# A new order for the first ten microseconds: q on one queue, f1id and w1's first piece on the other, longer warm-up with fillers, and the first filter visits at slots 4, 7, 10 and 13

## The chip, the cores and the metric

The kernel runs on one core of one Trainium2 chip. The metric is the device time of one execution in microseconds (us). The engines are named as the profile names them: PE (TensorE matmuls), PEld (its weight loads), DVE (VectorE), ACT (ScalarE), POOL (GpSimd) and SP (SyncE). DMAs are issued here from SP, ACT and POOL; "SPq" and "ACTq" are rows of DMA issues.

## The reference

Two branches read q, and their sum is added to q. `A` is a gated long convolution, `B` a two-layer perceptron with a Mish between the layers.

```python
x = A_q                                    # 1 x 2048 x 448
xn = _layernorm(x, axis=-1)
# _A_ref(xn, k, v, shift_k, ssm_k, ssm_D): 4-tap causal conv of k, times v,
# then a causal convolution over 2048 steps (by FFT) with ssm_k, plus kv * ssm_D, times xn
# _B_ref(xn, w1, b1, w2): h = xn @ w1 + b1 (448 -> 1792); act = mish(h); act @ w2 (1792 -> 448)
return x + _A_ref(xn, A_k, A_v, A_shift_k, A_ssm_k, A_ssm_D) + _B_ref(xn, B_w1, B_b1, B_w2)
```

## The kernel before, in words

**The perceptron sets the order.** The 2048 tokens are cut into 8 chunks of 256 (`NCHUNK`), the 1792 hidden columns into 7 groups of 256 (`NP`). One chunk with one group is a *pair*, 56 in all, chunk by chunk. Each matrix is kept as a high part and a low part (`w1h`/`w1l`, `w2h`/`w2l`, `XH`/`XL`, `ach`/`acl`), and each product is the sum of high x high, high x low and low x high. Pair i is worked in two *slots*: in slot 2i its first product (`g1_mm`, line 465, 22 matmuls), in slot 2i+1 its Mish and the split of the result (`mish`, lines 473, 74 and 75), followed on PE by the second product of pair i-2 (`g2_mm`, lines 490 to 492, 12 matmuls). The engines run what they are given in the order of the code.

**Chunk 0 splits the weights.** During chunk 0 each pair needs a new piece of w1 and, two pairs later, of w2. They come by DMA into a pool of four buffers (`kr`), where a load waits until an earlier piece has been split. `w1_hi` (ACT, line 342) writes the high part, `w1_lo` (lines 347 and 349, DVE) the low part; `split` (lines 74 and 75) does the same for w2. The p-th piece of w1 is split in slot 2p-2, the p-th piece of w2 after slot 2p+3.

**The convolution is sewn in by tables.** Its first Fourier stage takes 16 *visits*: 8 for the filter h (`H_AT`, slot of each) and 8 for k times v (`KV_AT`). A visit is `f1_mm` (line 125, 8 matmuls into two `pc` buffers in PSUM, of which there are two), then `f1_fold` (line 131: a copy by ACT; lines 132 and 134: an add and a subtract by DVE), and three slots later `f1_out` (line 140: two DMAs issued by ACT to the scratch `Dh` or `Dkv`). Where work is due in the same slot, the order of the tables' loops decides.

**The head** is what runs before slot 0, written by hand at lines 595 to 636. PE runs three warm-up matmuls that depend on constants alone. The two 128-token halves of chunk 0 of q are loaded: the first half by a 64-partition DMA from SP and one from ACT, the second by ACT. Then ACT issues `f1id` (the first stage's matrix and the identity for transposes), SP the first filter tile (h's group 1), w1's first piece in two parts, w1's second piece, `b1`, and h's group 2. DVE makes the statistics of each half (`stats`, `aggr`, `eps`), POOL the reciprocal root (`power`), DVE the normalized half (`norm`, `tail`). PE runs the visit of h's group 1 (`H_HEAD`) and then transposes each half (line 426); ACT writes `XH` (line 438), DVE `XL` (line 436). POOL makes the low part of the first part of w1's first piece. The visit's fold stands in slot 0 and its output in slot 3.

Of the kernel before, what the change touches and what calls it, by code (L numbers as in the profile page):

```python
# [7 lines left out]
F32 = mybir.dt.float32  # L8
# [7 lines left out]
NJ = 16  # L16
# [5 lines left out]
EPS = 1e-5  # L22

G2_LAG = 2
H_HEAD = 1
H_AT = {2: 4, 3: 8, 0: 12, 4: 16, 5: 20, 6: 26, 7: 32}
KV_AT = (24, 29, 34, 39, 44, 50, 55, 60)
H0_AT = 63
OCT_AT = (65, 3)
I2_AT = {98: (6, 7), 102: (0, 1), 106: (2, 3), 111: (4, 5)}  # L30
LATE = 2
WARM = 3
WARM_N = 448


@with_exitstack
def tile_kernel(ctx: ExitStack, tc, q, k, v, sk, hT, sD, w1, b1, w2, c_f1, c_g, c_gi, c_i2, out):
# [53 lines left out]
    def at(slot, fn, *args):  # L91
        plan.setdefault(int(slot), []).append((fn, args))
# [16 lines left out]
    def h_load(g, eng=None):  # L109
        HT[g] = xt()  # L110
        (eng or nc.sync).dma_start(HT[g], hT[:, 2 * g:2 * g + 2])
        if g == 0:
            dt = xt()[0:1, 0]
            nc.sync.dma_start(dt, sD)
            SD.append(dt)


    def f1_mm(src, g, key):
        x = src.pop(g)
        PS[key, g] = ps = [pc(), pc()]  # L120
        for b in range(2):
            for h in range(2):
                for jj in range(2):
                    rg = 32 * (2 * b + h)
                    nc.tensor.matmul(ps[h][64 * jj:64 * jj + 64, b, :D], f1[rg:rg + 32, 0:64], x[rg:rg + 32, jj],  # L125
                                     start=True, stop=True, tile_position=(rg, 64 * jj))
# [200 lines left out]
    RW = {}  # L327


    def w1_load(p, parts=((0, 2),)):  # L330
        if ("1", p) not in RW:
            RW["1", p] = kr().rearrange("p a b -> p (a b)").rearrange("p (n a b) -> p n a b", n=2, a=4)
        for a, b in parts:
            nc.sync.dma_start(RW["1", p][:, a:b], w1[p, :, a:b])

    def w1_parts(p, a, b):
        f = lambda t: t[:, :, 256 * p + 128 * a:256 * p + 128 * b].rearrange("p k (n b) -> p k n b", b=128)
# [27 lines left out]
    def ln_load(c, eng=None):  # L365
        Q[c] = mp.tile([128, 2, D], F32, name="qt", tag="qt", bufs=3)
        if c:
            nc.sync.dma_start(Q[c], q[:, 2 * c:2 * c + 2])
        else:
            for jj in range(2):  # L370
                for h, e in ((0, nc.sync), (64, nc.scalar)) if jj == 0 else ((0, nc.scalar),):
                    n = 128 if jj else 64
                    e.dma_start(Q[c][h:h + n, jj], q[h:h + n, jj])

    def ln_parts(c):
        st = mp.tile([128, 2, 6], F32, name="bst", bufs=2)
# [127 lines left out]
    def mlp_slot(s):  # L504
        i, half = divmod(s, 2)
        n = len(pairs)
        j = i - G2_LAG
        if half == 0:
            if i < n:
                c, p = pairs[i]  # L510
                if c + 1 < NCHUNK:
                    if p == 0:
                        ln_load(c + 1)
                    if p == (2 if c else 3):
                        ln_stats(c + 1)
                    if c == 0 or p == NP - 3:
                        dv(len(drip))
                    if p == NP - 2:
                        ln_norm(c + 1)
                    if p == NP - 1:  # L520
                        ln_T(c + 1, 1)
                g1_mm(i)
        else:
            if i < n:
                c, p = pairs[i]
                if p == NP - 2 and c + 1 < NCHUNK:
                    ln_T(c + 1, 0)
                mish(i)
            if 0 <= j < n - 1:
                g2_mm(j)  # L530
            elif j == n - 1:
                for jj in range(2):
                    g2_mm(j, (jj,))
                    g2_evac(pairs[j][0], (jj,))
# [3 lines left out]
    nslots = 2 * (len(pairs) + G2_LAG)  # L538

    for g, t in H_AT.items():  # L540
        if g != 2:
            at(t - 5 if t > 7 else t - 3, h_load, g)
        if g == 0:
            after(t - 2, lambda: V.tensor_add(HT[0][0:1, 0], HT[0][0:1, 0], SD.pop()))
        at(t, f1_mm, HT, g, "h")
        after(t, f1_fold, g, "h")
        at(t + 3, f1_out, Dh, g, "h")
# [49 lines left out]
    one = cp.tile([128, NJ], F32, name="one")  # L597
    V.memset(one, 1.0)
    ve0 = cp.tile([128, 2], F32, name="ve0")
    warm = g2p.tile([128, 512], F32, name="pg2")  # L600
    for _ in range(WARM):
        nc.tensor.matmul(warm[0:NJ, 0:WARM_N], one, one[:, 0:1].to_broadcast([128, WARM_N]), start=True, stop=True)
    ln_load(0)

    nc.scalar.activation(ve0, mhalf, AF.Mish)
    ve1 = cp.tile([128, 2], F32, name="ve1")
    nc.gpsimd.tensor_tensor(ve1, one[:, 0:2], mhalf, op=ALU.pow)
    nc.scalar.dma_start(f1id, c_f1)
    h_load(H_HEAD)
    w1_load(0, ((0, 1), (1, 2)))  # L610
    w1_load(1)
    nc.sync.dma_start(b1t, b1)
    h_load(2)
    stats, aggr, eps, power, norm, tail = ln_parts(0)
    for jj in range(2):
        stats(jj)
        aggr(jj)
        eps(jj, jj + 1)
        power(jj, jj + 1)
    f1_mm(HT, H_HEAD, "h")  # L620
    w1_hi(0, 0, 1)
    w1_lo(0, 0, 1, (nc.gpsimd, None))
    ps = [g2p.tile([128, 512], F32, name="pg2") for _ in range(2)]
    x_tiles(0)
    for jj in range(2):
# [1 line left out]
        tail(jj, jj + 1)  # L627
        transposes(0, jj, ps[jj])
        x_split(0, jj, ps[jj], 0)
    w1_hi(0, 1, 2)  # L630
    x_split(0, 0, ps[0], 1)
    w1_lo(0, 0, 1, (None, V))
    x_split(0, 1, ps[1], 1)
    w1_lo(0, 1, 2)
    plan2.setdefault(0, []).append((f1_fold, (H_HEAD, "h")))
    plan.setdefault(3, []).insert(0, (f1_out, (Dh, H_HEAD, "h")))
    for s in range(nslots):
        j = s // 2 - G2_LAG - 1
        if s % 2 == 0 and j >= 0 and pairs[j][1] == NP - 1:
# [69 lines left out]
```

## Time and profile before

| | us |
|---|---|
| median of 3 timed runs | 379.8 (379.71 to 380.72) |
| the profiled execution, its own time | 379.97 |
| its span, first to last instruction | 377.9 |
| PE busy | 364.6 (96%) |
| DVE busy | 266.6 (71%) |
| ACT busy | 177.1 (47%) |
| first matmul of pair 0 starts | 12.50 |

The span lies 2.1 us under the time of its own execution. Times inside the run are counted from the span's start. In a row of the timeline the first number is the start, the second the length, then the engine, the line of the code, the operation, the tile written and the tiles read, the number of instructions, and in brackets how long the engine had been idle before and what ended that.

### The profile page before, as it was taken

Reading aid. Unit: us, or ns where it says so; the run is one execution under the profiler, and the core shown is the slowest. Engines: PE = TensorE matmul, PEld = TensorE weight load, DVE = VectorE, ACT = ScalarE, POOL = GpSimd, SP = SyncE. Lnnn points to the kernel's source line nnn. Section 1 sums busy time; section 2 is a strip of 40 time slices with the busy share of each in tenths; the row PEclk is TensorE's granted clock in tenths of the full one; section 3 lists DMA queues with packets and bytes.
Section 4 is the critical chain, followed back from the end, with each engine's and each line's share of the span. In section 5 each row is a group of like instructions: output and inputs, shape, how many; then the busy total and the mean of one; then the engine's idle time right before and its main releaser. Section 6 shows DMA issues by size and latency. Waiting matters only on the chain.

```text
span 377.9 us, 7967 instructions
## 1 busy us (share of the span) xinstructions
PE 364.6 (96%) x3382; PEld 295.0 (78%) x3382; DVE 266.6 (71%) x355; ACT 177.1 (47%) x298; POOL 25.1 (7%) x42
## 2 busy tenths in 40 slices
PE   5999999999999999999999999999999999999993
PEld 1788888978888988988886666666666889888982
DVE  2889758999999998997434747654564822997741
ACT  2677743454334433533453646456555435224540
POOL 2101000000020001000010000110000012111110
PEclk9899999999999999999999999999999999999999
DMA  7799986839488427513875498878494468739927
GB/s 265 269 310 337 378 309 178 250 85 298 116 293 216 112 52 256 152 46 97 258 254 192 143 300 225 251 256 237 129 305 121 117 182 329 260 122 295 199 63 145
DMA packets 31987, 79.38 MB, mean 210 GB/s; under 512 B 2897, under 2 KB 18130, under 8 KB 31954
## 3 DMA queue, kind: packets, MB, share of 16 engines
q1 hardware_dynamic: 20754, 47.22, 36.8%
q10 hardware_dynamic: 9328, 22.50, 22.6%
q0 software_dynamic: 1872, 9.18, 8.9%
q8 instruction: 26, 0.43, 0.5%
q14 instruction: 7, 0.06, 0.0%
HBM read 50.44 MB, written 28.44 MB: 209 GB/s over the span
## 4 chain that ended last, share of the span: by engine, by line
PE 86%; DMA 4%; DVE 3%; ACT 3%; issue 1%; ACTq 1%; SPq 0%
PE pg L465 34%; PE pg L490 12%; PE pg L491 11%; PE pg L492 11%; PE pc L199 7%; PE pc L244 4%; PE pc L125 4%; PE pg L426 2%; PE pc L302 2%; DMA f1id<-in_c_f_dram 2%; DMA Dkv<-st 1%; DMA av<-Dkv 1%; ACT a L473 1%; DVE st L132 1%; ACT XH L438 0%
## 5 line engine op out<-in xcount | busy, mean ns | idle before, releaser
L473 ACT ACTIVATE a<-pg,b1t 128x256 f32<-128x256 f32 x112 | 47.1, 472 | 107.0 <-PE pg L465 88.3
L465 PE MATMUL pg<-XH,w1h 128*128 128x256 f32 x448 | 91.2, 285 | 0.7 <-ACT XH L438 0.7
L490 PE MATMUL pg<-w2h,ach 128*128 128x448 f32 x224 | 83.3, 372 | 0.2 <-DVE qt L497 0.2
L465 PEld LDWEIGHTS pg<-XH,w1h 128*128 128x128 f32 x448 | 69.7, 188 | 17.7 <-issue 15.1
L491 PE MATMUL pg<-w2l,ach 128*128 128x448 f32 x224 | 81.4, 363 | 0.6 <-DVE w2l L75 0.6
L492 PE MATMUL pg<-w2h,acl 128*128 128x448 f32 x224 | 81.4, 363 | 0.0
L75 DVE TENSOR_TENSOR acl<-a,ach 128x512 fp32r<-128x512 f32 x56 | 38.4, 687 | 58.0 <-ACT ach L74 57.8
L465 PE MATMUL pg<-XL,w1h 128*128 128x256 f32 x448 | 69.7, 277 | 0.2 <-DVE XL L436 0.2
L465 PEld LDWEIGHTS pg<-XL,w1h 128*128 128x128 f32 x448 | 59.4, 188 | 0.3 <-DVE XL L436 0.3
L465 PE MATMUL pg<-XH,w1l 128*128 128x256 f32 x336 | 56.9, 278 | 0.0
L490 PEld LDWEIGHTS pg<-w2h,ach 128*128 128x128 f32 x224 | 42.0, 187 | 12.7 <-issue 9.8
L465 PEld LDWEIGHTS pg<-XH,w1l 128*128 128x128 f32 x336 | 46.9, 188 | 0.0
L491 PEld LDWEIGHTS pg<-w2l,ach 128*128 128x128 f32 x224 | 42.1, 188 | 3.5 <-DVE w2l L75 1.2
L492 PEld LDWEIGHTS pg<-w2h,acl 128*128 128x128 f32 x224 | 42.1, 188 | 2.7
L74 ACT CAST ach<-a 128x512 fp32r<-128x512 f32 x56 | 34.7, 620 | 1.8
L163 DVE TENSOR_TENSOR x<-x 128x896 f32<-128x896 f32 x24 | 26.2, 1091 | 0.8
L438 ACT CAST XH<-pg 128x512 fp32r<-128x512 f32 x16 | 9.4, 588 | 30.2 <-PE pg L426 29.1
L436 DVE TENSOR_TENSOR XL<-pg,XH 128x512 fp32r<-128x512 f32 x16 | 11.0, 688 | 16.8 <-ACT XH L438 16.7
L393 POOL TENSOR_TENSOR shift<-mv,mone 128x2 f32<-128x2 f32 x7 | 2.8, 396 | 280.1 <-DVE mv L385 280.1
L131 ACT COPY st<-pc 128x896 f32<-128x896 f32 x16 | 14.5, 909 | 13.4 <-PE pc L125 13.3
L125 PE MATMUL pc<-x,f1id 32*64 32x448 f32 x256 | 17.3, 585 | 3.3 <-DMA f1id<-in_c_f_dram 3.3
L252 ACT COPY qe<-pc 128x896 f32<-128x896 f32 x16 | 13.7, 911 | 13.5 <-PE pc L244 13.0
(66 smaller groups left out, 396.5 us busy)
## 6 DMA issues: line engine op xcount, KB each, us to landing
Dh<-st ACTq DMA_DIRECT2D x16, 448.0 KB, 5.3
Dkv<-st ACTq DMA_DIRECT2D x16, 448.0 KB, 5.1
ah<-Dh SPq DMA_DIRECT2D x8, 896.0 KB, 6.9
av<-Dkv SPq DMA_DIRECT2D x8, 896.0 KB, 6.7
E<-qe ACTq DMA_DIRECT2D x16, 448.0 KB, 4.9
e<-E POOLq DMA_DIRECT2D x7, 896.0 KB, 8.7
kr<-in_k_dram SPq DMA_DIRECT2D x10, 448.0 KB, 6.9
x<-in_hT_dram SPq DMA_DIRECT2D x8, 448.0 KB, 6.1
```

What stands on the lines that cost most here:

```text
L74: nc.scalar.copy(h, raw)
L75: V.tensor_sub(l, raw, h)
L125: nc.tensor.matmul(ps[h][64 * jj:64 * jj + 64, b, :D], f1[rg:rg + 32, 0:64], x[rg:rg + 32, jj], start=True, stop=True, tile_position=(rg, ...
L131: nc.scalar.copy(st[:, 1], o)
L163: V.tensor_add(KV[g], KV[g], o)
L199: nc.tensor.matmul(p[32 * t:32 * t + 32, r, :D], g[rs, t, c], a[rs, t], start=True, stop=True, tile_position=(64 * r, 32 * t))
L244: nc.tensor.matmul(ps[t // 2][cg:cg + 32, t % 2, :D], gi[ts, r, c, 32 * jj:32 * jj + 32], Y[o][c][ts, r], start=c == 0, stop=c == 1, tile_ ...
L465: nc.tensor.matmul(ps[:, n], l, r, start=n_ == 0, stop=n_ == len(mm) - 1)
L473: nc.scalar.activation(a[:, n], ps[:, n], AF.Mish, bias=b1t[:, 2 * p + n:2 * p + n + 1])
L490: nc.tensor.matmul(ps, ah[:, n, cs], w2h[:, f], start=f == 0, stop=False)
L491: nc.tensor.matmul(ps, ah[:, n, cs], w2l[:, f], start=False, stop=False)
L492: nc.tensor.matmul(ps, al[:, n, cs], w2h[:, f], start=False, stop=f == NF - 1)
```

## The change

In the head, SP now issues both halves of chunk 0 of q, each as one DMA of 128 partitions. ACT issues `f1id` and the first part of w1's first piece; SP issues the second part behind q. The filter tile of group 1 moves behind `b1` in SP's queue. The visit of group 1 leaves the head: `H_AT` now puts groups 1, 2, 3 and 0 at slots 4, 7, 10 and 13; they stood in the head and at slots 4, 8 and 12. The warm-up is four matmuls of 448 columns and one of 128; after the transposes of the first half a filler matmul of 64 columns runs, after those of the second half two of 128. The warm-up writes a `pc` buffer, no longer a `pg2` buffer. Both parts of w1's first piece are cast by ACT before `XH`, and both low parts are made by DVE. The load of chunk 1 of q moves from slot 0 to slot 2.

```diff
-H_HEAD = 1
-H_AT = {2: 4, 3: 8, 0: 12, 4: 16, 5: 20, 6: 26, 7: 32}
+H_AT = {1: 4, 2: 7, 3: 10, 0: 13, 4: 16, 5: 20, 6: 26, 7: 32}
...
-WARM = 3
-WARM_N = 448
+WARM = (448,) * 4 + (128,)
+FILL = ((64,), (128, 128))
...
             for jj in range(2):
-                for h, e in ((0, nc.sync), (64, nc.scalar)) if jj == 0 else ((0, nc.scalar),):
-                    n = 128 if jj else 64
-                    e.dma_start(Q[c][h:h + n, jj], q[h:h + n, jj])
+                nc.sync.dma_start(Q[c][:, jj], q[:, jj])
...
-                    if p == 0:
+                    if p == (0 if c else 1):
                         ln_load(c + 1)
...
-        if g != 2:
-            at(t - 5 if t > 7 else t - 3, h_load, g)
+        if g != 1:
+            at(t - 5 if t > 7 else t - 4, h_load, g)
...
-    warm = g2p.tile([128, 512], F32, name="pg2")
-    for _ in range(WARM):
-        nc.tensor.matmul(warm[0:NJ, 0:WARM_N], one, one[:, 0:1].to_broadcast([128, WARM_N]), start=True, stop=True)
+    warm = pc()
+
+    def heat(ns):
+        for n in ns:
+            nc.tensor.matmul(warm[0:NJ, 0, 0:n], one, one[:, 0:1].to_broadcast([128, n]), start=True, stop=True)
+
+    heat(WARM)
     ln_load(0)
-
+    nc.scalar.dma_start(f1id, c_f1)
+    w1_load(0, ((0, 1, nc.scalar), (1, 2, nc.sync)))
...
-    nc.scalar.dma_start(f1id, c_f1)
-    h_load(H_HEAD)
-    w1_load(0, ((0, 1), (1, 2)))
     w1_load(1)
     nc.sync.dma_start(b1t, b1)
-    h_load(2)
+    h_load(1)
...
-    f1_mm(HT, H_HEAD, "h")
     w1_hi(0, 0, 1)
-    w1_lo(0, 0, 1, (nc.gpsimd, None))
+    w1_hi(0, 1, 2)
...
         x_split(0, jj, ps[jj], 0)
-    w1_hi(0, 1, 2)
+        heat(FILL[jj])
+    w1_lo(0, 0, 1)
     x_split(0, 0, ps[0], 1)
-    w1_lo(0, 0, 1, (None, V))
     x_split(0, 1, ps[1], 1)
     w1_lo(0, 1, 2)
-    plan2.setdefault(0, []).append((f1_fold, (H_HEAD, "h")))
-    plan.setdefault(3, []).insert(0, (f1_out, (Dh, H_HEAD, "h")))
```

What stands on an engine in a row is shown at three places; the changed kernel's line numbers are 3 or 4 lower behind the edits. First SP's queue at the start, before (`qt` is q, `x` a filter tile, `kr` a piece of w1 or w2, `b1t` the bias):

```order
L373 DMA qt<-in_q_dram 64x448
L111 DMA x<-in_hT_dram 128x896
L334 DMA kr<-in_w_dram 128x512 x2
L334 DMA kr<-in_w_dram 128x1024
L612 DMA b1t<-in_b_dram 128x14
L111 DMA x<-in_hT_dram 128x896
```

The same place after the change:

```order
L370 DMA qt<-in_q_dram 128x448 x2
L333 DMA kr<-in_w_dram 128x512
L333 DMA kr<-in_w_dram 128x1024
L611 DMA b1t<-in_b_dram 128x14
L110 DMA x<-in_hT_dram 128x896
L356 DMA kr<-in_w_dram 128x896
```

The filter tile that stood second has moved behind the bias, and both halves of q stand first. Second, DVE from the end of the head to the split of pair 0, before (`w1h` and `w1l` in lines 347 and 349 are the low parts of w1, `st` is the fold of a visit, `acl` the low part of a Mish result):

```order
L436 TENSOR_TENSOR XL<-pg_145,XH 128x4x128
L349 TENSOR_TENSOR w1h<-kr,w1h 64x128
L436 TENSOR_TENSOR XL<-pg_146,XH 128x4x128
L347 TENSOR_TENSOR w1l<-kr,w1h 128x3x128
L349 TENSOR_TENSOR w1h<-kr,w1h 64x128
L347 TENSOR_TENSOR w1l<-kr,w1h 128x3x256
L349 TENSOR_TENSOR w1h<-kr,w1h 64x256
L132 TENSOR_TENSOR st<-pc,st 128x896
L134 TENSOR_TENSOR st<-pc,st 128x896
L75 TENSOR_TENSOR acl<-a,ach 128x512
```

The same place after the change:

```order
L346 TENSOR_TENSOR w1l<-kr,w1h 128x3x128
L348 TENSOR_TENSOR w1h<-kr,w1h 64x128
L433 TENSOR_TENSOR XL<-pg_134,XH 128x4x128
L433 TENSOR_TENSOR XL<-pg_135,XH 128x4x128
L346 TENSOR_TENSOR w1l<-kr,w1h 128x3x128
L348 TENSOR_TENSOR w1h<-kr,w1h 64x128
L346 TENSOR_TENSOR w1l<-kr,w1h 128x3x256
L348 TENSOR_TENSOR w1h<-kr,w1h 64x256
L74 TENSOR_TENSOR acl<-a,ach 128x512
```

One more low part of w1 stands ahead of the two `XL`, and the two operations of a fold are gone from ahead of `acl`. Third, DVE between the low parts of w2's second piece (p = 1) and third piece (p = 2), before:

```order
L75 TENSOR_TENSOR w2l<-kr,w2h 128x896
L347 TENSOR_TENSOR w1l<-kr,w1h 128x3x256
L349 TENSOR_TENSOR w1h<-kr,w1h 64x256
L382 BN_STATS bst<-qt 128x6 x2
L385 BN_AGGR mv<-bst 128x2 x2
L388 TENSOR_SCALAR ve<-mv 128x2
L75 TENSOR_TENSOR acl<-a,ach 128x512
L75 TENSOR_TENSOR w2l<-kr,w2h 128x896
```

The same place after the change:

```order
L74 TENSOR_TENSOR w2l<-kr,w2h 128x896
L346 TENSOR_TENSOR w1l<-kr,w1h 128x3x256
L348 TENSOR_TENSOR w1h<-kr,w1h 64x256
L379 BN_STATS bst<-qt 128x6 x2
L382 BN_AGGR mv<-bst 128x2 x2
L385 TENSOR_SCALAR ve<-mv 128x2
L74 TENSOR_TENSOR acl<-a,ach 128x512
L131 TENSOR_TENSOR st<-pc,st 128x896
L133 TENSOR_TENSOR st<-pc,st 128x896
L74 TENSOR_TENSOR w2l<-kr,w2h 128x896
```

The fold of the visit at slot 7 (group 2) now stands between them. Before, a fold stood in slots 0, 4, 8 and 12; now one stands in slots 4, 7, 10 and 13.

More of the change, by code (lines that the diff above doesn't have):

```diff
@@ L327, in tile_kernel, with w1_load @@
     RW = {}
-    def w1_load(p, parts=((0, 2),)):
+    def w1_load(p, parts=((0, 2, nc.sync),)):
         if ("1", p) not in RW:
             RW["1", p] = kr().rearrange("p a b -> p (a b)").rearrange("p (n a b) -> p n a b", n=2, a=4)
-        for a, b in parts:
-            nc.sync.dma_start(RW["1", p][:, a:b], w1[p, :, a:b])
+        for a, b, eng in parts:
+            eng.dma_start(RW["1", p][:, a:b], w1[p, :, a:b])
     def w1_parts(p, a, b):
```

## The prediction

> **What bounds the kernel now.** The page comes first. Its busy times and its 40 slices (9.4 us each, digits are tenths) show a PE that is full from the second slice to the last but one.
>
> ```profile
> PE 364.6 (96%) x3382; PEld 295.0 (78%) x3382; DVE 266.6 (71%) x355; ACT 177.1 (47%) x298; POOL 25.1 (7%) x42
> ...
> PE   5999999999999999999999999999999999999993
> ```
>
> So the time is PE's stream of work, plus what PE waits for. The change touches the first slice and the spacing of the visits up to slot 13; I read that stretch only. The timeline, PE's rows, first: warm-up, the head's visit, the transposes, the first matmul of pair 0, the first wait of the second product, the first matmul of pair 3.
>
> ```profile
> 1.00 4.17 PE L602 MATMUL pg<-one 128*16 128x448 f32 x6 [1.00 <-DVE one L598]
> ...
> 8.43 1.80 PE L125 MATMUL pc<-x,f1id 32*64 32x448 f32 x16 [3.26 <-DMA f1id<-in_c_f_dram]
> 10.17 1.66 PE L426 MATMUL pg<-f1id,xn 128*128 128x128 f32 x8
> 12.50 0.62 PE L465 MATMUL pg<-XH,w1h 128*128 128x256 f32 x3 [0.68 <-ACT XH L438]
> ...
> 23.06 0.47 PE L491 MATMUL pg<-w2l,ach 128*128 128x448 f32 x1 [0.63 <-DVE w2l L75]
> ...
> 25.37 0.52 PE L465 MATMUL pg<-XH,w1h 128*128 128x256 f32 x3
> ```
>
> Pair 0 starts at 12.50. What it waits for stands in DVE's and POOL's rows.
>
> ```profile
> 3.77 0.63 DVE L382 BATCH_NORM_STATS2 bst<-qt 128x6 f32<-128x448 f32 x1 [2.82 <-DMA qt<-in_q_dram]
> ...
> 7.64 0.63 DVE L382 BATCH_NORM_STATS2 bst<-qt 128x6 f32<-128x448 f32 x1 [2.85 <-DMA qt<-in_q_dram]
> ...
> 9.55 1.18 DVE L404 TENSOR_SCALAR xn<-qt,mv,rstd 128x448 f32<-128x448 f32 x1 [0.22 <-POOL rstd L394]
> 10.76 0.20 DVE L408 COPY xn<-xn 128x64 f32<-128x64 f32 x1
> ```
>
> ```profile
> 8.76 0.75 POOL L394 TENSOR_TENSOR rstd<-ve,mhalf 128x1 f32<-128x1 f32 x1 [3.33 <-DVE ve L388]
> 9.48 1.00 POOL L347 TENSOR_TENSOR w1l<-kr,w1h 128x384 fp32r<-128x384 f32 x1
> ```
>
> The second half of q ends the head. It is there at 7.64; then come statistics, POOL's root, the second half's normalization (1.18 us, beside POOL's 1.00 us of low part; the same instruction takes 0.51 us for the first half), its tail to 10.96, transposes, ACT's cast, pair 0: 12.50 - 7.64 = 4.86 us.
>
> ```profile
> 8.60 0.51 DVE L404 TENSOR_SCALAR xn<-qt,mv,rstd 128x448 f32<-128x448 f32 x1
> ```
>
> Last, the chain of waits gives PE's units where nothing is late: a first product is 2.51 us, a visit 0.94, and the second product what lies between, 53.46 - 51.06 = 2.40.
>
> ```profile
> 48.55 2.51 PE pg L465 x22
> ...
> 53.46 0.94 PE pc L125 x16
> ```
>
> **Part 1: when q is there.** ACT issued the second half early, and it landed 6.2 us later.
>
> ```profile
> 0.75 1.46 ACTq L373 DMA_DIRECT2D qt<-in_q_dram  x2
> ...
> 1.37 0.56 SPq L111 DMA_DIRECT2D x<-in_hT_dram  x1
> ```
>
> ```profile
> qt<-in_q_dram ACTq DMA_DIRECT2D x1, 224.0 KB, 6.2
> ```
>
> Why: from 3.5 to 4 us the DMA engines served one queue alone, and that was the larger one, SP's, with the filter tile. ACT's queue has no row there.
>
> ```profile
> q1 hardware_dynamic: 32, 0.11, 74.4%
> ```
>
> In the changed order the two halves of q (448 KB, 459 kB in thousands of bytes) have only `f1id` (128 KB, 131 kB) beside them: 590 kB. The rates at that time are the last number of these rows:
>
> ```profile
> 2.00:3.00 1.00, 1.00 (x2) 0.15 (x1) 0.00 (x0) 0.76 (x1) 0.00 (x0) 1.00 1.04 253
> 3.00:4.00 1.00, 1.00 (x3) 0.18 (x2) 0.23 (x1) 0.73 (x2) 0.00 (x0) 1.00 0.84 203
> 4.00:5.00 1.00, 1.00 (x3) 0.11 (x1) 0.73 (x3) 0.00 (x0) 0.12 (x1) 1.00 0.87 312
> ```
>
> 253 + 203 = 456 kB by 4.0, the other 134 at 312 by 4.43. From the last byte to the start of the statistics I take 0.55 us; for the first half before (229 kB, by 2.91, used at 3.77) the same sum gives 0.86, with other bytes mixed in. So the second half is used at 5.0 (an estimate; 4.6 if the two queues mix less, 5.8 in a rival below) and not at 7.64.
>
> **Part 2: from q to pair 0.** The 4.86 us shrink in two places. POOL no longer makes a low part beside the normalization: 1.18 becomes 0.51, so -0.67. And the transposes: before, eight took 1.66 us at half clock. PE's granted clock (the third number from the end; PE's busy time is the first after the length) shows why:
>
> ```profile
> 4.55:7.97 3.42, 0.63 (x2) 0.00 (x0) 0.54 (x3) 0.14 (x1) 0.55 (x1) 1.00 1.02 376
> 7.97:11.38 3.41, 2.95 (x22) 1.58 (x23) 2.63 (x7) 0.55 (x2) 1.72 (x2) 0.50 1.04 402
> 11.38:14.79 3.41, 2.58 (x20) 2.15 (x19) 2.73 (x6) 3.35 (x5) 0.00 (x0) 1.00 0.52 210
> ```
>
> A stretch with 0.63 of 3.42 us busy was followed by clock 0.50; one with 2.95 busy was followed by 1.00. After the change the warm-up ends near 6.0 (six passes took 4.17 us; 8.5 are issued, the later ones at full clock), and the transposes of the first half and a filler come at 6.7: about 2.3 of the 3.42 us are busy. That is nearer to the 2.58 after which the clock stayed than to 0.63, so I take full clock: the last four transposes take 0.4 and not 0.8 us, -0.3. Rest: 4.86 - 0.67 - 0.3 = 3.9. Pair 0 starts at 5.0 + 3.9 = 8.9, **-3.6 us**. The visit that leaves the head costs nothing there: the transposes that count are those of the second half, at 11.0, after it. The casts of w1 by ACT and the extra low part on DVE (384 columns on POOL in 1.00 us, less on DVE) lie in the wait for the transposes and the cast; without that cover they would cost up to 1 us. The Trainium skill (TensorE: Matmul & The Clock Gate, The HAM clock gate) says that the half rate returns after an idle window of some 3.4 us; the trace shows it returning after a window that was not idle, 18% busy, so the trace is stricter, and the fillers have a purpose.
>
> **Part 3: the visit in the stream.** The visit of group 1 ran while PE had nothing else. At slot 4 it is in the full stream: **+0.94**.
>
> **Part 4: the stretch up to pair 3.** From 12.50 to 25.37 are 12.87 us. Three first products, a visit and a second product are 7.53 + 0.94 + 2.40 = 10.87, so 2.0 us are lost. The fold of the head's visit and its output stand in this stretch: ACT issues the output's two DMAs just ahead of the Mish of pair 1.
>
> ```profile
> 18.18 1.31 ACTq L140 DMA_DIRECT2D Dh<-st  x2
> ...
> 19.54 0.84 ACT L473 ACTIVATE a<-pg,b1t 128x256 f32<-128x256 f32 x2 [1.30 <-PE pc L125]
> ...
> 21.91 1.09 DVE L75 TENSOR_TENSOR w2l<-kr,w2h 128x896 fp32r<-128x896 f32 x1 [0.15 <-ACT w2h L74]
> ```
>
> Then come the split, the cast of w2, and at 23.00 the low part on which PE waits (the row at 23.06). With fold and output gone from here, that chain is, from the end of pair 1: 0.2 to start (an estimate), 21.91 - 19.54 = 2.37 for Mish, split and cast, 1.09 for the low part = 3.66; PE has a visit, a first product and one matmul (0.94 + 2.51 + 0.20 = 3.65) to do in that time. It fits. What stays is 0.2 for `XL` in pair 0 (DVE makes an extra low part first) and 0.1 at each change of shape: 0.5. **-1.5.**
>
> **Part 5: the new wait.** Between the ends of the low parts of w2's pieces 0 and 2, DVE took, before,
>
> ```profile
> 24.36 1.09 DVE L132 TENSOR_TENSOR st<-pc,st 128x896 f32<-128x896 f32 x1
> 25.48 1.09 DVE L134 TENSOR_TENSOR st<-pc,st 128x896 f32<-128x896 f32 x1
> ...
> 31.64 1.08 DVE L75 TENSOR_TENSOR w2l<-kr,w2h 128x896 fp32r<-128x896 f32 x1
> ```
>
> 32.72 - 23.00 = 9.7 us with one fold. After the change two folds (slots 4 and 7) stand there: 9.7 + 2.2 = 11.9. PE needs, in the same time, the rest of a second product (2.2), two first products, a visit, a second product and one matmul: 2.2 + 5.02 + 0.94 + 2.40 + 0.2 = 10.8. So pair 2's second product waits about 1.1 us for `w2l`, and with it everything on PE behind it; 1.3 with the changes of shape. Before, the stretch from 25.37 to 36.59 (11.22 us for 5.02 + 4.80 + 0.94 = 10.76) lost 0.46. **+0.85.**
>
> Behind slot 13 both kernels have done the same visits, and the tables are the same.
>
> **Sum.** -3.6 + 0.94 - 1.5 + 0.85 = -3.3 us, from the profiled execution's 379.97 to 376.7; from the median, 379.8, to **376.5**.
>
> **Rivals.** *The queues share evenly.* Then `f1id` and w1's first part (384 KB, 393 kB) move beside q: 852 kB; 768 by 5.0, the rest at 312 by 5.27, used at 5.8. That is 0.8 later: 377.3. For it: both of ACT's transfers are now issued at the start. Against it: the half microsecond in which ACT's queue had no byte. The Trainium skill (DMA: Bandwidth & Descriptors, Issuing engines are not separate DMA queues) says that transfers of all issuers run on the same 16 engines and interleave, so that a second issuer saves issue time only; by that rule alone the sum is this rival's. The same page (Queues, rings and completion order) has each engine drain a whole packet of one ring before it turns to the next, which agrees with the row at 3.5 us.
>
> *The clock stays at half* to 11.38, as before. The last transposes take 0.4 more, pair 0 starts at 9.3, and its first 2.1 us run at half rate, 1.05 lost: +1.45, 377.95. It decides if 2.3 busy us of a window are too few, or the window falls otherwise.
>
> *The load stream is the bound.* The DMA share (last but one) is near full behind the head:
>
> ```profile
> 12.50:25.37 12.87, 12.09 (x94) 10.56 (x95) 11.41 (x17) 10.40 (x17) 0.00 (x0) 1.00 0.77 258
> 25.37:36.59 11.22, 11.22 (x85) 9.69 (x84) 10.99 (x18) 7.86 (x12) 1.71 (x3) 1.00 0.97 330
> 36.59:48.39 11.80, 11.80 (x94) 10.49 (x92) 9.20 (x12) 9.07 (x16) 0.00 (x0) 1.00 0.99 368
> ```
>
> If loads set the pace, they come earlier only by idle time that goes: 0.23 x 12.87 = 3.0 us in the first row. With half of it kept (buffers come free no sooner), the gain is 1.5: 378.3. Against it: PE is busy all through the two rows below.
>
> *Slower: w1's fifth piece.* ACT casts it in slot 6, in front of the Mish of pair 3, the cast of w2's third piece and so the `w2l` of part 5.
>
> ```profile
> 20.15 0.33 SPq L334 DMA_DIRECT2D kr<-in_w_dram  x1
> ...
> 26.98 1.05 ACT L342 CAST w1h<-kr 128x1024 fp32r<-128x1024 f32 x1 [1.12 <-DMA kr<-in_w_dram]
> ```
>
> Before, it took 6.8 us, and ACT waited 1.12. It is issued when DVE frees its buffer, 7.65 us behind the start of pair 0; now about 6.7, since a fold no longer stands ahead: 15.6. ACT wanted it at 26.98 - 1.12 = 25.86, 13.4 behind pair 0; now, by part 4, 1.5 less: 20.8. DVE is behind by then, which gives some 0.6 of grace (an estimate); from 21.4 each us of lateness is a us of PE. At 6.8 us again that is 1.0 (377.5, within my range); slower than 379.8 by 0.3% needs a landing 10.2 us or more after the issue (25.8, 4.4 us past 21.4). The longest load of that pool before took 8.8:
>
> ```profile
> DMA to landing us min/median/max: 3.7/6.3/8.8
> ```
>
> *It does not do what it says:* the second half of q comes no sooner. Then pair 0 starts at 7.64 + 3.9 = 11.5, -1.0, and the sum is -0.7: 379.1, no change to be told. Against it: q is first in its queue.
>
> **Chances.** Forecast 0.55, even queues 0.15, clock 0.12, loads 0.07, slower 0.03, no sooner 0.08. A difference of 0.3%, 1.1 us, is about what a measurement can tell from none. Faster: the first four, 0.89; same 0.08; slower 0.03. Range: below, 4.6 for q and half of the new wait (-0.4 - 0.55), so 375.5; above, the clock's 378.0 with w1's or the loads' case beyond it: 375.5 to 378.2.
>
> **What would show it.** In the changed profile: DVE's second statistics at 4.6 to 5.3; its second normalization 0.5 us; transposes 0.1 us apart; pair 0 at 8.6 to 9.4 with clock 1.00; no ACT wait ahead of the Mish of pair 1; a PE wait of about 1 us on `w2l` in pair 2's second product, some 19 us behind the start of pair 0; SP's third to sixth loads without gaps. I am wrong if pair 0 starts after 10, or if PE loses over 2 us between pair 0 and slot 13.

## The result and the profile after

The changed kernel took 376.8 us (median of 4 runs, 376.71 to 376.92). The kernel before, run beside it, took 380.26 (379.71 to 381.4). The ratio is 0.9905, with a 95% interval of 0.988 to 0.9931: 3.5 us sooner, where 376.5 was forecast. The profiled execution is the one of 376.92, with a span of 374.9; it is compared below with the profiled execution of before (379.97, span 377.9). Two single executions among all the runs, one of 1252.29 us of the kernel before and one of 920.61 us in experiment 6, stand far outside and enter no ratio.

The page: PE's first slice now reads 8 and not 5, and the rest of the row is as full as it was.

```profile
PE 365.5 (97%) x3392; PEld 295.5 (79%) x3392; DVE 266.1 (71%) x356; ACT 176.9 (47%) x298; POOL 23.8 (6%) x41
...
PE   8999999999999999999999999999999999999993
```

DVE's rows of the head: statistics of the first half, statistics of the second half, normalization of the second half.

```profile
3.92 0.63 DVE L379 BATCH_NORM_STATS2 bst<-qt 128x6 f32<-128x448 f32 x1 [2.96 <-DMA qt<-in_q_dram]
...
4.96 0.63 DVE L379 BATCH_NORM_STATS2 bst<-qt 128x6 f32<-128x448 f32 x1
...
6.86 0.51 DVE L401 TENSOR_SCALAR xn<-qt,mv,rstd 128x448 f32<-128x448 f32 x1 [0.22 <-POOL rstd L391]
```

The row at 4.96 has no bracket: DVE came straight from its own work on the first half, which ended at 4.94. q had only just landed. Its second half was issued at 1.17, and the longer of the two landings of q took 3.8 us (3.76 in the trace, so 4.93):

```profile
DMA to landing us min/median/max: 3.1/3.5/3.8
```

So the landing and DVE met within 0.01 us, and from there on the chain runs through DVE. What the DMA engines moved up to then stands in the next rows: the rate in two stretches (last number), and SP's queue (q1) and ACT's (q10) from 0 to 4.43 us, in packets, MB and share of the engines' time.

```profile
3.00:4.00 1.00, 1.00 (x3) 0.18 (x2) 0.09 (x1) 0.17 (x1) 0.00 (x0) 1.00 1.07 388
4.00:5.00 1.00, 1.00 (x4) 0.31 (x3) 0.92 (x4) 0.00 (x0) 0.00 (x0) 1.00 1.06 388
...
q1 hardware_dynamic: 284, 0.46, 35.8%
q10 hardware_dynamic: 232, 0.31, 18.8%
```

SP's queue had begun the last packets of q's 0.46 MB by 4.43. In the same time ACT's had come to 0.31 MB: `f1id` (0.13) and 0.18 of w1's first part.

PE's rows: the warm-up, the transposes of each half (four in 0.66 us, against 1.12 at half clock in experiment 1), pair 0, pair 3, the wait in pair 2's second product, the visit at slot 10.

```profile
1.00 4.92 PE L601 MATMUL pc<-one 128*16 128x448 f32 x10 [1.00 <-DVE one L595]
6.46 0.66 PE L423 MATMUL pg<-f1id,xn 128*128 128x128 f32 x4 [0.55 <-DVE xn L401]
...
7.42 0.66 PE L423 MATMUL pg<-f1id,xn 128*128 128x128 f32 x4
...
8.75 0.63 PE L462 MATMUL pg<-XH,w1h 128*128 128x256 f32 x3
...
20.21 0.52 PE L462 MATMUL pg<-XH,w1h 128*128 128x256 f32 x3
...
29.62 0.47 PE L488 MATMUL pg<-w2l,ach 128*128 128x448 f32 x1 [0.38 <-DVE w2l L74]
...
32.03 1.01 PE L124 MATMUL pc<-x,f1id 32*64 32x448 f32 x16
```

The table of windows, cut where the clock's record has its boundaries (the clock is the third number from the end): both stretches of the head are at 1.00.

```profile
4.08:7.49 3.41, 2.78 (x14) 1.02 (x13) 2.98 (x10) 1.57 (x3) 1.30 (x2) 1.00 1.05 350
7.49:10.90 3.41, 3.28 (x24) 2.68 (x25) 3.29 (x8) 1.79 (x3) 0.00 (x0) 1.00 0.92 369
```

ACT's rows: the casts of w1's first part, and the Mish of pair 1.

```profile
5.30 1.29 ACT L341 CAST w1h<-kr 128x512 fp32r<-128x512 f32 x2 [2.14 <-DMA kr<-in_w_dram]
...
14.28 0.84 ACT L470 ACTIVATE a<-pg,b1t 128x256 f32<-128x256 f32 x2
```

The Mish has no wait ahead of it, as part 4 asked, and the casts are over before the transposes of the first half end. SP's third to sixth loads stand without a gap, as asked; later ones do not:

```profile
1.64 0.90 SPq L333 DMA_DIRECT2D kr<-in_w_dram  x2
2.58 0.43 SPq L611 DMA_DIRECT2D b1t<-in_b_dram  x1
3.06 0.43 SPq L110 DMA_DIRECT2D x<-in_hT_dram  x1
...
4.46 6.43 SPq L333 DMA_DIRECT2D kr<-in_w_dram  x2
```

The last row is two of w1's pieces over 6.43 us; no engine's wait goes back to it. One sign came out otherwise: PE's wait for `w2l` is 0.38 us in its row and 0.55 in the distances, where about 1 was expected, and it stands 20.9 us behind the start of pair 0, not 19.

Followed along the starts of the pairs, the two profiled executions differ like this: pair 0 at 8.75 and not 12.50, -3.75; pair 3 at 20.21 and not 25.37, so another -1.41 on the way; pair 8 at 50.97 and not 54.33, which gives back 1.80. From there the distance stays between 3.3 and 3.5 to pair 26. Then 0.46 is given back between pairs 26 and 27 and 0.42 between pairs 48 and 49, so that the last pair starts 2.50 sooner. Behind the start of the last pair 0.5 is gained: 3.0 in the span. That last stretch took 17.5 us here and 18.0 before, and lies anywhere from 17.0 to 18.2 in the fourteen profiles of this case, so its 0.5 can't be put down to the change. The first of the two late losses has its rows on DVE and PE:

```profile
146.37 1.09 DVE L153 TENSOR_TENSOR x<-kr,skb 128x896 f32<-128x896 f32 x1 [1.61 <-DMA kr<-in_k_dram]
```

```profile
159.10 0.39 PE L462 MATMUL pg<-XH,w1h 128*128 128x256 f32 x1 [0.30 <-DVE XL L433]
```

DVE waits 1.61 us for a piece of k (1.24 before), and its `XL` comes 0.3 us late for pair 27.

### The profile page after: what moved, and what is told of

It reads as the page before. It is cut to its first block, busy times and chain, and to the rows that moved or that the text cites. A ratio compares the mean times of both kernels' runs of the same rounds, so it can differ in the third digit from the quotient of the medians.

```text
span 374.9 us, 7980 instructions
## 1 busy us (share of the span) xinstructions
PE 365.5 (97%) x3392; PEld 295.5 (79%) x3392; DVE 266.1 (71%) x356; ACT 176.9 (47%) x298; POOL 23.8 (6%) x41
## 4 chain that ended last, share of the span: by engine, by line
PE 83%; DVE 8%; ACT 3%; DMA 2%; issue 2%; POOL 0%; SPq 0%; DVEq 0%; ACTq 0%
PE pg L462 34%; PE pg L487 11%; PE pg L489 10%; PE pg L488 10%; PE pc L198 7%; PE pc L243 4%; PE pc L124 3%; PE pc L301 2%; PE pg L423 2%; DMA kr<-in_k_dram 2%; DVE acl L74 1%; DVE x L162 1%; DVE st L131 1%; ACT a L470 1%; DMA qt<-in_q_dram 1%
## 5 line engine op out<-in xcount | busy, mean ns | idle before, releaser
L131 DVE TENSOR_TENSOR st<-pc,st 128x896 f32<-128x896 f32 x16 | 17.4, 1087 | 4.3 <-ACT st L130 4.0
```

What stands on the lines that cost most here:

```text
L131: V.tensor_add(st[:, 0], e, st[:, 1])
```

## The experiments

All times are medians of whole runs. The kernel before was run again beside each group: 380.36 beside the first four, 380.67 beside the next four, 380.74 beside the last four. Ratios are to these. The last group (experiments 2, 5 and 10) ran on another chip than the first two. The changed kernel itself was not run again, so a distance to its 376.8 is one between sessions, and the kernel before moved by up to 0.5 us between them.

**1. The order of the loads alone.** The changed kernel with the head's loads of before:

```diff
-                nc.sync.dma_start(Q[c][:, jj], q[:, jj])
+                for h, e in ((0, nc.sync), (64, nc.scalar)) if jj == 0 else ((0, nc.scalar),):
+                    n = 128 if jj else 64
+                    e.dma_start(Q[c][h:h + n, jj], q[h:h + n, jj])
...
+    nc.scalar.dma_start(f1id, c_f1)
+    h_load(1)
+    w1_load(0, ((0, 1, nc.sync), (1, 2, nc.sync)))
```

> The changed kernel, with its head's loads issued as before the change: q's first half by SP and ACT, its second half by ACT, f1id by ACT behind them, the filter tile second in SP's queue. Theory (the order in which the loads are served sets when q's second half is used): the second statistics start at 7.5 to 7.7 instead of 4.96, pair 0 at 11.2 to 11.6 instead of 8.75, and the time rises by 2.4 to 2.8 us, to 379.2 to 379.6. Rival (the stream of weight loads behind the head sets the pace, so that the head's delay is mostly taken up later): less than 1.5 us more, below 378.3.

Measured: 380.69 (12 runs), ratio 1.0007 (0.999 to 1.0023). The whole gain is gone, 3.9 us. DVE's rows and the windows:

```profile
7.36 0.63 DVE L381 BATCH_NORM_STATS2 bst<-qt 128x6 f32<-128x448 f32 x1 [2.53 <-DMA qt<-in_q_dram]
...
9.26 0.51 DVE L403 TENSOR_SCALAR xn<-qt,mv,rstd 128x448 f32<-128x448 f32 x1 [0.22 <-POOL rstd L393]
```

```profile
10.24 1.12 PE L425 MATMUL pg<-f1id,xn 128*128 128x128 f32 x4
```

```profile
5.50:8.91 3.41, 1.16 (x6) 0.32 (x4) 1.45 (x5) 1.17 (x2) 0.44 (x1) 1.00 1.03 380
8.91:12.32 3.41, 3.41 (x15) 2.01 (x15) 2.60 (x7) 1.58 (x4) 0.32 (x1) 0.50 0.56 226
```

The second half is back at 7.36, 2.4 later, and pair 0 starts at 12.25. The other 1.1 us is the clock: the longer wait leaves a window with 1.16 us of PE work in it, and the next is at 0.50. Over half of the 1.1 is the fillers, which stand in the way at that rate: the last transposes start 0.98 us behind the second normalization and not 0.56, since a filler runs until then, and pair 0 starts 0.2 later behind its cast. The rival of a bounding load stream asked for under 378.3 and falls. My own number was short by a us, because I had not carried the clock into it. The edit changes several things at once (the first half in two DMAs of 64 partitions, the second half on ACT, the filter tile ahead); experiments 2 and 3 test the last two one at a time, and no run tests the first.

**2. Bytes ahead of q's second half.** The changed kernel, with the filter tile of group 1 issued by SP between the halves of q:

```diff
                 nc.sync.dma_start(Q[c][:, jj], q[:, jj])
+                if not jj:
+                    h_load(1)
```

> The kernel after, with the load of filter group 1 (448 KB) issued by SP between the two halves of q, as SP's second issue; q stays on SP. Theory (q's second half is served in turn behind what stands ahead of it in its queue, and 448 KB at some 0.3 MB per us are 1.5 us): second statistics at 6.2 to 6.7 in the place of 4.96, pair 0 at 10.0 to 10.5, the clock perhaps lost as well, time 378.0 to 379.5. Rival (bytes ahead don't count, q comes at the same time; or only the time of issue counts, 0.45 us): second statistics by 5.5, time within 0.6 of the kernel after.

Measured: 378.28 (377.42 to 379.18, 6 runs), ratio 0.9942 (0.9926 to 0.9959). The second statistics, and the window:

```profile
6.46 0.63 DVE L381 BATCH_NORM_STATS2 bst<-qt 128x6 f32<-128x448 f32 x1 [1.51 <-DMA qt<-in_q_dram]
```

```profile
4.97:8.38 3.41, 1.80 (x9) 0.70 (x7) 1.60 (x6) 1.23 (x2) 1.30 (x2) 1.00 1.05 398
```

The half comes 1.5 us later for 448 KB ahead of it; pair 0 starts at 10.26, 1.51 later, and the time is 1.5 longer. Here the clock held, so this is the price of 448 KB ahead in the same queue by itself, and the theory has its number.

**3. Which queue.** The changed kernel, with q's second half issued by ACT, first in ACT's queue:

```diff
-                nc.sync.dma_start(Q[c][:, jj], q[:, jj])
+                (nc.scalar if jj else nc.sync).dma_start(Q[c][:, jj], q[:, jj])
```

> The kernel after, with the second half of q issued by ACT, first in its queue, and the first half alone on SP. Theory (what counts is that q stands first on its queue and that no larger transfer is beside it, not which queue it is on): second statistics at 4.9 to 5.2, time within 0.3 of 376.8. Rival (a queue of ACT's is served late in any case): second statistics at 6 or later, pair 0 1 us or more later, 377.8 or more.

Measured: 377.93 (377.15 to 379.58, 9 runs), ratio 0.9928 (0.9906 to 0.9951): 1.1 more than the changed kernel. DVE's second statistics, and ACT's rows behind them:

```profile
5.06 0.62 DVE L379 BATCH_NORM_STATS2 bst<-qt 128x6 f32<-128x448 f32 x1
```

```profile
7.95 1.14 ACT L341 CAST w1h<-kr 128x512 fp32r<-128x512 f32 x2 [4.31 <-DMA kr<-in_w_dram]
```

```profile
kr<-in_w_dram ACTq DMA_DIRECT2D x1, 256.0 KB, 6.3
```

q was there in time, as the theory had it. Its forecast of the whole time was wrong all the same: w1's first part, now third in ACT's queue, landed 6.3 us after its issue and not 4.1. ACT casts it ahead of `XH`, so its first cast starts at 7.95 (5.30 in the changed kernel), and pair 0 at 10.11 and not 8.75. The cast starts 2.65 us later for 224 KB more ahead in its queue; at experiment 2's price that would be 0.75, so bytes ahead in the own queue are not the whole of it here, and what else delays it is not shown. The rival saw the right size for the wrong transfer. The head has two transfers of this rank: q's second half and w1's first part.

**4. The warm-up, shortened.** The changed kernel with `WARM = (448,) * 3` and no fillers.

> The changed kernel with three warm-up matmuls of 448 columns as before and no fillers; nothing else. Theory (PE's clock falls to half after a stretch of 3.4 us that is mostly idle, and the longer warm-up with fillers keeps it up): warm-up ends near 5, the stretch up to 7.5 holds about 1.7 busy us of 3.4; if that is too little, the transposes of the second half are 0.2 us apart, pair 0 starts at 9.1 to 9.3 and runs at half rate to about 10.9, and the time rises by 0.8 to 1.4 us; between the runs it varies by 0.5 us or more, as the stretches fall by chance. Rival (the transposes alone keep the clock up, the fillers do nothing): within 0.2 us of 376.8.

Measured: 378.82 (377.52 to 379.74, 7 runs), ratio 0.9956 (0.9937 to 0.9975), 2.0 more.

```profile
4.99:8.40 3.41, 1.72 (x9) 0.84 (x8) 3.00 (x9) 2.11 (x4) 1.28 (x2) 1.00 1.05 356
8.40:11.82 3.42, 3.06 (x14) 3.07 (x15) 3.31 (x6) 1.25 (x2) 0.00 (x0) 0.50 0.77 268
```

Pair 0 starts at 8.76, as with the long warm-up, but takes 4.03 us and not 2.83. The theory has the direction and place, and was low by 0.6 or more. But the profile does not account for the 2.0. It is of the fastest of the seven runs (377.52, 0.6 above the profiled changed kernel). It loses 1.2 in pair 0 and another 0.9 between pairs 5 and 6, where PE waits 0.47 us for `XL`, and has half of that back by the last pair. One of the seven runs kept a mean clock of 0.998, as high as the changed kernel's, and took 378.82 as well. So the fall of the clock costs 1.2 us in the profile where it is seen, and the rest of the 2.0 is open.

**5. The fillers alone.** The changed kernel with the long warm-up and `FILL = ((), ())`.

> The kernel after, without the filler matmuls behind the transposes; the long warm-up stays. Theory (the fillers keep the window between warm-up and pair 0 busy enough): in some runs the clock falls to 0.50 in the head, as with the short warm-up, and those are 2 us longer: median 377.0 to 378.8, spread over 1 us. Rival (the warm-up up to 5.9 alone holds the clock; the fillers are 0.3 us of work that changes nothing): 376.8 within 0.2, spread as the kernel after's.

Measured: 376.41 (6 runs: four from 376.02 to 376.5, two at 377.5), ratio 0.99 (0.9885 to 0.9915).

```profile
4.10:7.51 3.41, 2.48 (x11) 0.82 (x9) 2.99 (x9) 1.38 (x3) 1.30 (x2) 1.00 1.03 365
```

The clock held in the profiled run, and the median is not longer than with fillers. The long warm-up is what counts. Two of six runs were 1.2 longer, where the changed kernel's four lie within 0.2. Their mean clocks, 0.997 and 0.995, are no lower than those of the other four (0.995 to 0.998), so a fall of the clock is not what sets them apart; what does is not known.

**6. The warm-up in the kernel before.** The kernel before with `WARM = 7`, nothing else.

> The kernel before, with seven warm-up matmuls in the place of three. Theory (the window with little work behind the warm-up makes the clock fall): no window of the head at 0.50, the last eight transposes take 0.9 and not 1.66 us, the visit 0.9 and not 1.8; pair 0 at 12.0 to 12.2 and not 12.50, since it waits on q; the median falls by 0.3 to 0.8 and the spread of the runs from 1.7 to under 1. Rival (the clock falls whatever the warm-up does, by a fixed time since the start): clock 0.50 again, time the same.

Measured: 379.51, ratio 0.9969 (0.995 to 0.9988); eleven of twelve runs lie from 379.14 to 380.16, while 25 runs of the kernel before beside it spread from 378.64 to 382.58. The mean clocks of the eleven are 0.994 to 0.999, those of the 25 0.981 to 0.996.

```profile
8.81 1.01 PE L125 MATMUL pc<-x,f1id 32*64 32x448 f32 x16
...
12.01 0.61 PE L465 MATMUL pg<-XH,w1h 128*128 128x256 f32 x3 [0.67 <-ACT XH L438]
```

The visit takes 1.01 and not 1.80 us, pair 0 starts 0.49 sooner, and the time falls by 1.2, more than the 0.3 to 0.8 expected. So a warm-up alone would have given a third of the gain, and taken most of the spread away.

**7. The low part on POOL.** The changed kernel with the first of w1's low parts on POOL again.

```diff
+        w1_lo(0, 0, 1, (nc.gpsimd, None))
...
-    w1_lo(0, 0, 1)
+    w1_lo(0, 0, 1, (None, V))
```

> The changed kernel, with the 384 columns of low part of w1's first part made by POOL again, beside the second normalization. Theory (the two slow each other): the second normalization takes 1.1 to 1.2 us instead of 0.51, pair 0 starts 0.6 to 0.7 later, at 9.4, XL comes no later than now relative to it, and the time rises by 0.3 to 0.7 us, to 377.1 to 377.5. Rival (the 1.18 us of before came from something else, such as the DMA traffic at that time): the normalization stays at 0.5 us and the time within 0.2 of 376.8, or falls by up to 0.2 since DVE has less ahead of XL.

Measured: 377.19 (376.44 to 377.47, 5 runs), ratio 0.9913 (0.9895 to 0.9931), 0.4 more.

```profile
6.87 1.18 DVE L401 TENSOR_SCALAR xn<-qt,mv,rstd 128x448 f32<-128x448 f32 x1 [0.21 <-POOL rstd L391]
```

```profile
6.81 0.99 POOL L346 TENSOR_TENSOR w1l<-kr,w1h 128x384 fp32r<-128x384 f32 x1
```

DVE's normalization starts 0.06 behind POOL's subtraction and ends 0.25 behind it: 1.18 us in place of 0.51, and pair 0 at 9.44, 0.69 later. The Trainium skill (SBUF — State Buffer, SBUF: two separate sides) describes a port pair that VectorE and GpSimd share as an exclusive lock: for some kinds of VectorE operation the one that starts first has it for its whole instruction, and the other blocks until then. The rows agree in direction and not in full. POOL still had 0.93 us to run; blocked for all of that, the normalization would have ended near 8.31 (7.80 + 0.51), and it ended at 8.05, having lost 0.67.

**8. The spacing of the visits.** The changed kernel with visits at slots 4, 8, 11, 14 and 17.

```diff
-H_AT = {1: 4, 2: 7, 3: 10, 0: 13, 4: 16, 5: 20, 6: 26, 7: 32}
+H_AT = {1: 4, 2: 8, 3: 11, 0: 14, 4: 17, 5: 20, 6: 26, 7: 32}
```

> The changed kernel with the visits of groups 1, 2, 3, 0 and 4 at slots 4, 8, 11, 14 and 17 instead of 4, 7, 10, 13 and 16. Theory (the wait of pair 2's second product for w2's low part comes from the fold of the visit at slot 7, ahead of it on DVE): the wait of 0.4 to 0.6 us is gone, later low parts have room, and the time falls by 0.3 to 0.6 us, to 376.2 to 376.5. Rival (DVE is behind as a whole, and the wait moves to the next low part of w2 or w1, or a visit now waits for its buffers): the time stays within 0.2 of 376.8 or rises.

Measured: 376.82 (376.61 to 377.13, 4 runs), ratio 0.9904 (0.9882 to 0.9925): no change. The waits of PE still hold the row

```profile
PE pg L488 <- DVE w2l L74: 0.5, 1, 0.5
```

but it belongs to a later pair: pair 4 to pair 5 took 5.02 us with no loss, pair 6 to pair 7 took 6.86, and pair 9 began at 56.05 (56.00 in the changed kernel). Pair 10 began 0.45 later than in the changed kernel, which the last stretch of this profile (17.05 us for 17.52) gives back. The rival was right: the fold only makes another low part late.

**9. What is late, done first.** The changed kernel, with the split of w2's piece registered ahead of the fold where both fall in one slot (slots 7 and 13):

```diff
+    for p in range(NP):
+        after(2 * (p + G2_LAG) - 1, w2_split, p)
...
-        after(2 * (p + G2_LAG) - 1, w2_split, p)
```

> The kernel after, with the split of w2's piece registered ahead of the fold where both fall in one slot (slots 7 and 13), so that DVE makes the low part of w2's piece 2 ahead of the second fold. Theory (the prediction's part 5: the two folds make that low part late): the wait at 29.62 goes, pair 3 to the visit at slot 10 takes some 11.1 and not 11.8 us, the time falls by 0.3 to 0.6. Rival (as when the visits stood at slots 8, 11, 14: the low part that comes next is late instead): pair 8 at the same time as before the edit, no change.

Measured: 375.89 (375.17 to 376.84, 6 runs), ratio 0.9879 (0.9849 to 0.9908), 0.9 less than the changed kernel. DVE's order (of the fold its first row only) and PE's second product of pair 2; first the changed kernel's DVE rows, then the experiment's.

```profile
26.36 1.08 DVE L131 TENSOR_TENSOR st<-pc,st 128x896 f32<-128x896 f32 x1
28.49 1.08 DVE L74 TENSOR_TENSOR w2l<-kr,w2h 128x896 fp32r<-128x896 f32 x1
```

```profile
26.58 1.08 DVE L74 TENSOR_TENSOR w2l<-kr,w2h 128x896 fp32r<-128x896 f32 x1
27.59 1.08 DVE L131 TENSOR_TENSOR st<-pc,st 128x896 f32<-128x896 f32 x1
```

```profile
29.30 0.36 PE L488 MATMUL pg<-w2l,ach 128*128 128x448 f32 x1
```

The low part now ends at 27.66, PE needs it at 29.30, and the wait is gone: pair 3 to the visit at slot 10 takes 31.59 - 20.43 = 11.16 us and not 11.82, 0.66 less. No later wait took its place: the waits of PE hold no `w2l` any more. The theory stands for this place. For the whole time its 0.3 to 0.6 was low: five of the six runs lie under the changed kernel's lowest, 376.71. The two ratios' intervals overlap, though, and the give-back at pair 26 was missing from this profile, as from most (experiment 10).

**10. The load of k.** The changed kernel with k's loads two slots earlier, and the same with the edit of experiment 9 as well:

```diff
-        at(t - d - (3 if g > 1 else 2), k_load, g)
+        at(t - d - (5 if g > 1 else 2), k_load, g)
```

> The kernel after, with the loads of k two slots earlier in SP's queue, so that the one that DVE waited 1.6 us for is no longer issued behind the chunk's output. Theory (the 0.4 us that the kernel after loses at pair 26 are that load, issued behind an output that holds SP for 22 us): that DVE wait and PE's wait for XL at 159.1 go, time lower by 0.3 to 0.5. Rival (the loss at pair 26 is chance of one profiled run; it was not there in two experiments): the time is the same within 0.2.

> The kernel after, with both edits: w2's split ahead of the fold in slots 7 and 13, and k's loads two slots earlier. Theory: the gain of the split alone (0.9 by the medians) and 0.3 more, 375.5 to 375.8. Rival (the k load costs nothing any more once DVE is not late): the same as the split alone, 375.9 within 0.2.

Measured: 376.91 (376.87 to 377.21, 4 runs), ratio 0.9908 (0.9895 to 0.9921), and 376.14 (375.38 to 377.74, 6 runs), ratio 0.9887 (0.9868 to 0.9907). The first:

```profile
144.67 1.08 DVE L153 TENSOR_TENSOR x<-kr,skb 128x896 f32<-128x896 f32 x1
```

DVE no longer waits there, pair 27 starts at 158.55 and not 159.10, and the last pair 0.43 sooner. But the span is 375.0, since what follows the start of the last pair took 18.0 us and not 17.5; what sets that stretch is not settled. The time agrees with the rival, no change. Nor does the trace credit the edit: pair 26 to pair 27 took 5.72 us here, but also, within 0.01, in seven of the eight experiments on the changed kernel that leave k's loads alone (6.26 in the changed kernel, 6.44 in experiment 8). In experiments 5 and 9 DVE waited 1.07 and 0.85 us for the same piece, and PE lost nothing. So the loss is one of some executions, as the rival had it, and the edit's own worth is not shown. Run together on one chip, the two kernels here differ by the order of split and fold alone: 0.8 us, and five of six runs of the second lie under the lowest of the first. That is the second sight of experiment 9's gain. Experiment 9 by itself stays the best version, 375.89; with the k loads added it is no better.

**11. The output of the head's visit, in the kernel before.** It stands in slot 6 and not in slot 3:

```diff
-    plan.setdefault(3, []).insert(0, (f1_out, (Dh, H_HEAD, "h")))
+    plan.setdefault(6, []).insert(0, (f1_out, (Dh, H_HEAD, "h")))
```

> The kernel before, with one edit: the output of the head's visit (two DMAs issued by ACT, 1.31 us) stands in slot 6 and not in slot 3. Theory (the prediction's part 4: these issues, ahead of pair 1's Mish, make w2's first low part late): Mish of pair 1 starts some 1 us sooner than 19.54, the first low part of w2 ends near 22, PE's wait at 23.06 (0.63 to 0.9) goes, pair 0 to pair 3 takes 12.0 to 12.2 instead of 12.87, the time falls by 0.5 to 0.9. Rival (the lost time of that stretch is that of the fold and of slow first matmuls, ACT's issue is covered): no change of the stretch, time within 0.2.

Measured: 381.65 (379.89 to 383.52, 12 runs), ratio 1.0032 (1.0007 to 1.0056): slower by 1.0, against both theories. Its windows, and ACT's rows:

```profile
4.67:8.08 3.41, 0.56 (x2) 0.00 (x0) 0.14 (x1) 0.00 (x0) 0.55 (x1) 1.00 1.00 345
8.08:11.49 3.41, 2.08 (x18) 0.71 (x19) 2.83 (x7) 0.62 (x1) 1.72 (x2) 0.50 1.02 357
11.49:14.91 3.42, 2.74 (x13) 2.34 (x12) 2.06 (x5) 2.35 (x4) 0.00 (x0) 0.50 0.63 252
```

```profile
28.36 4.95 ACTq L140 DMA_DIRECT2D Dh<-st  x2
33.35 0.84 ACT L473 ACTIVATE a<-pg,b1t 128x256 f32<-128x256 f32 x2 [4.77 <-DVE ve L388]
```

Two things lie over each other. In this profile (382.96, well above the median) the loads of an unchanged head came 0.7 to 1 us later and the clock stayed at 0.50 until 18.3, which shifts pair 0 by 1.3 to 13.79 and pair 1 by 2.9 to 18.50; the edit, in slots 3 and 6, stands behind that. The edit's own effect is in the distances. Pair 2 to pair 3 took 5.03 us and not 6.15, and the Mish of pair 1 starts 2.80 us behind the start of its pair and not 3.94 (2.70 in the changed kernel): the wait of part 4 went, as the theory says. But the next visit's output, 28.36, now held ACT for 4.95 us and not 1.24. In the record of its two issues, the second waits for a completion semaphore that a load of w1 carries as well, the one that SP issued at 26.15:

```profile
26.15 0.33 SPq L334 DMA_DIRECT2D kr<-in_w_dram  x1
```

Loads of that line took a median of 6.6 us to land in this run, which gives 32.75; the second issue went out at 32.73. So pair 3 to pair 8 took 30.63 us and not 28.96. In the kernel before the same issue waits for the same semaphore, but there the head's output had used it last, and that had landed 2.1 us earlier. So the issue that was moved left its completion semaphore to another transfer, and the next output had to wait for that one. The gain of 1.1 was given back as 1.7.

## Why the prediction was right, step by step

**Part 1, q.** Used at 4.96 where 5.0 was forecast, landed at 4.93, its bytes through by 4.43 as worked out. The 0.55 from the last byte to use had no row behind it (the one row beside it gave 0.86), and 0.53 came of it. That the bytes come out is luck in part, since two misjudgements cancel. The sum let q share with `f1id` alone, 0.59 MB by 4.43. In the trace 0.77 MB had gone by then, because ACT's queue had taken 0.18 MB of w1's first part as well. And the sum took rates of 253, 203 and 312 GB/s from before for the stretch from 2 to 5 us, where 191, 388 and 388 came. From 3 to 5 us the two queues moved 0.42 and 0.35 MB. So the sharing was close to what the rival of even queues had; its time, 5.8, is out because it used the same low rates. Experiments 1 and 2 put a price on the order: 2.4 us for the old one, 1.5 for 448 KB ahead. The rival of no gain asked for 7.64 and falls.

**Part 2, from q to pair 0.** 8.75 - 4.96 = 3.79 where 3.9 was worked out. The term for POOL, 0.67, is 0.69 in experiment 7 at pair 0, and 0.4 in the time. The clock held, with 2.78 us of the window busy where I had estimated 2.3. The step from that estimate to "full clock" leaned on the nearest of two rows, 0.63 and 2.58, far apart; in the head of experiments 2 and 4, windows of 1.80 and 1.72 now stand on the two sides. The clock's rival was priced at 1.45; where it comes true, in experiment 4, the profile shows 1.2 in pair 0 and the median 2.0. The sentence that the fillers have a purpose is not borne out: without them the clock held (experiment 5), and at half clock they stand in the way (experiment 1).

**Part 3 and part 5, the visit and the new wait.** Together 1.79 forecast, 1.80 measured between pairs 3 and 8; that it fits so closely is luck. Within it the wait is smaller: PE lost 0.55 at 29.62, and 0.66 came back in experiment 9, where about 1.1 was worked out. DVE's side was right (11.84 us between the two low parts; 11.9 forecast). PE's side was not: the sum let PE's need begin when w2's first low part ended, as it did before, when PE waited for that part. Now PE came to it later: the part ends at 17.73, PE uses it at about 18.0 and is ready for the next one at 29.07 (28.87 and one matmul of 0.2), 11.34 us behind 17.73 and not 10.8. That next one ends at 29.57, so 0.5 is left. The 0.25 that makes up for this lies between pairs 5 and 7, and what it is stays open.

**Part 4.** -1.41 for -1.5. Experiment 11 shows the mechanism by its local distances, 1.1 us between pairs 2 and 3 and as much ahead of the Mish of pair 1, though its whole time says nothing of it.

**The rivals.** The load stream is not the bound: experiment 1 loses the whole gain by the order of loads with the same bytes. w1's fifth piece was issued at 15.74 and cast at 20.50 with no wait ahead; that rival had no occasion.

**The sum.** Up to pair 8, where the sum ends, -3.3 was worked out and -3.36 measured. For the profiled execution 376.7 was worked out and 376.92 measured, and that owes something to luck: neither the two steps behind slot 13 that lose 0.4 each nor the 0.5 gained behind the last pair were in the sum. "Behind slot 13 both kernels have done the same visits, and the tables are the same" holds for the tables, not for the waits. The first step stands in two of the eleven profiles of the changed kernel and its variants, the second in seven; what brings them is not shown. The base moved too: the kernel before ran at 380.3 to 380.7 in the later comparisons and not at 379.8, and by those the gain is 3.5 to 3.9.

## What to carry to other kernels

In a head that waits for a load, list the transfers by who needs them first and put each at the front of a queue of its own rank. Experiment 2 prices a wrong place at the bytes ahead of it, experiment 3 at more than that. A forecast of a landing needs the rate as well as the order: here the rate rose from 203 and 312 to 388 GB/s with the new order. When a fixed order of work makes one engine late at a known point, swap what it does there before moving what surrounds it: moving the visits gave nothing, swapping split and fold gave 0.8 to 0.9. Check a moved DMA issue for what it waits for, not only for what it takes.

## What the runs showed of the hardware

**The clock's border.** Each run's clock record has boundaries 3.41 us apart. Of the windows of the head, those with 0.56, 0.63, 1.16 and 1.72 us of PE work were followed by 0.50, those with 1.80, 2.48, 2.78 and more by 1.00. That looks like a border at about half of a window. But a late window of experiment 7 does not fit it: 1.56 us of PE work, and the next window, with none, still at 1.00.

```profile
367.42:370.83 3.41, 1.56 (x8) 1.13 (x6) 1.25 (x2) 0.00 (x0) 0.00 (x0) 1.00 1.06 197
370.83:374.24 3.41, 0.00 (x0) 0.00 (x0) 0.00 (x0) 0.00 (x0) 0.00 (x0) 1.00 0.39 139
```

So the fall was seen up to 1.72 and the stay from 1.56 on, and busy time, whose matmul ends are modelled, does not by itself tell which of the two comes between. A half-rate window with 2.95 or more was followed by full rate, those with 2.08 and 2.74 (experiment 11) by another at half. The Trainium skill (TensorE: Matmul & The Clock Gate, The HAM clock gate) has a free-running window of 3413 ns and asks for an idle one before the rate falls; the length agrees, and the runs show that the rate can fall after a window that was half busy.

**The spread of the runs goes with the clock in part.** The window's boundary in the head lay anywhere from 3.66 to 5.94 us in the profiled runs, so windows fall otherwise in each run. The kernel before spread by 3.9 us over 25 runs, and by 1.0 with the longer warm-up beside it (eleven runs). Of the 25, the six with a mean clock under 0.984 took 380.85 to 382.58, the nine from 0.99 up 378.64 to 381.81: a loose tie. The changed kernel and experiment 8 spread by 0.2 and 0.5, over four runs each. But experiment 9 and the second kernel of experiment 10 spread by 1.7 and 2.4, over six, with the clock at full in their profiled runs. So the clock is not all of it, and the rest is open.
